# A finer-grained opening: 128-token pieces, half products ahead of the scores, and class-1 norms drained in three parts

## Chip, cores and metric

The kernel runs on 1 core of one Trainium2 chip. The metric is the device time of one execution in microseconds (us), lower is better, as the median of several executions. The kernel before takes 1280.66 us (three executions, 1279.89 to 1280.86).

## The reference

Two layers, each an attention block followed by a token-mixing MLP, with layer norms without weights, in bf16. Cut to what matters here:

```python
x = A_x                                  # 1 x 2048 tokens x 1024
for layer in range(2):
    h = layernorm(x)
    q, k, v = split(h @ wqkv)            # 32 heads of 32
    # 8 keys per query, 2 tokens apart: tokens t, t-2, ..., t-14 (masked below 0)
    logits = einsum("hsd,hswd->hsw", q, kg) * scale
    x = x + (softmax(logits) applied to vg) @ wo
    h = layernorm(x)
    x = x + MLP over the token axis(h)   # w1, gelu, w2, biases
```

The dilation of 2 splits the tokens into two classes that never meet in attention: even tokens (class 0) and odd ones (class 1), 1024 tokens or eight tiles of 128 each.

## The kernel before: the parts that matter

TensorE is the engine that is nearly always busy. The program fixes the order of each engine's instructions when it is built, and in the traces below an engine stands at an instruction whose operand isn't ready (1.24 us at 39.65 in the kernel before) rather than taking a later one. The schedule: two pieces of code make it.

The first is the opening: eight class-0 tiles are loaded, normed, transposed on TensorE ("turn"), copied from PSUM ("place"), and projected to q and k. Matmuls of the identity ("idle") fill TensorE meanwhile, for the sake of its clock: in the trace the first eight start about 0.43 us apart, the last eight about 0.21.

```python
        idle(16)
        moments(0)            # statistics on VectorE, 1/sqrt on ScalarE
        own_sum(0)
        moments(1)
        norm(0)
        turn(0)
        idle(3)
        # ... (cut: tiles 1 to 3, then the first projections, 256 tokens at a time)
        for u, i in (((1, 0), 2), ((1, 1), 3), ((0, 0), None)):
            banks[u] = bank()
            project(*u, 0, banks[u], 0, 2 * P)
```

Scores: for each feature tile, q times the shifted k on VectorE (the product T, 128x4096), which TensorE then sums over features with a selection matrix (the "sc" matmuls). In the first group of scores each T is followed by its own sum:

```python
            for par in range(2):
                ...
                T = self.t_buf(n, dq, par)
                mult = nc.vector.tensor_tensor(out=T, in0=q..., in1=window(k, ...), op=ALU.mult)
                ...
                if not joined:
                    self.qk_sum(dq, par, T)
```

The second piece weaves other work into this lead stream while the program is built. `second` is the class-1 norms (eight pieces), `v_ahead` the v projections of class 1 (sixteen pieces of 8 matmuls), `out0` the first output projection, and so on. The weave keeps its own count of TensorE and VectorE time, `pe` and `dve`, and pulls filling pieces in where that count says that TensorE would otherwise wait:

```python
    def weave(lead, fills, lags):
        ...
                u = next(fills[f], None)
                if u is not None:
                    pe = max(pe, opened[f]) + u[0]
                    dve += u[1]
                    return True
                del opened[f]
                when[f] = pe + lags.get(f, 6.0)        # the fill has ended: what follows it may open
                for x, y in (("out0", "partials"), ("out0", "late"), ("second", "v_ahead")):
                    if f == x and y in opened:
                        opened[y] = when[f]
        ...
            elif kind == "drain":
                while unit[0] in opened:               # all that is left of this fill, here and now
                    pull(True)
        ...
        weave(lead, {"second": second_class(), "v_ahead": v_ahead(), "out0": ..., ...},
              {"second": 25.0} if first else {})
```

In the stream of the attention:

```python
            yield from lead if lead is not None else qk_proj(0, 0)      # the opening
            yield "open", "second"
            if lead is not None:
                yield "drain", "second"                                 # all eight class-1 norms
            yield "open", "v_ahead"
            for n in range(last + 1):                                   # scores, softmax, p*v ...
```

Weights come through a pool of five buffers (`wbp`), which the v projections and the output projection share.

## Time and profile before

| | before |
|---|---|
| median | 1280.66 us (1279.89 to 1280.86) |
| profiled span | 1278.8 us, granted clock 1.0 |
| TensorE busy | 98% |
| TensorE idle in 0-12 / 12-34 / 34-60 / 60-180 / 180-242 us | 3.7 / 0.2 / 1.5 / 0.7 / 2.8 us |
| first projection / end of the first six | 11.98 / 25.61 us |
| first scores / second | 37.80 / 39.65 us (1.24 us of waiting before the second) |

The idle times are the length of a stretch less its "PE" column in the view by stage. The prediction shows that view, the waits and the order of work, so they aren't repeated here. One habit is needed for the rest: a row of the timeline reads "start, length, engine, line, operation, output<-inputs, shapes, count", and the bracket is the idle time of that engine just ahead of the row with what ended it.

### The profile page before, as it was taken

To read this page: it belongs to the slowest core of one execution; us is meant where nothing else is said; L and a number is where in the kernel's file an instruction comes from. 1 tells how busy PE (TensorE), PEld (TensorE's weight loads), DVE (VectorE), ACT (ScalarE), POOL (GpSimd) and SP (SyncE) were. 2 spreads that over 40 slices of the span, in tenths; PEclk is the share of its full clock that TensorE was granted. 3 is DMA by queue.
4 is the path that set the end of the run, shared out by engine and by line. 5 is a ranking of instruction groups with operands and counts; after the bars stand their busy time and mean duration, and the time that the engine had idled before them with its cause. 6 is when DMAs were issued, how large, how long until landed. Compare 5 with 4: busy or idle time off the path is not lost.

```text
span 1278.8 us, 15455 instructions
## 1 busy us (share of the span) xinstructions
PE 1258.0 (98%) x6163; PEld 577.4 (45%) x6284; DVE 689.9 (54%) x869; ACT 489.3 (38%) x812; POOL 61.3 (5%) x166
## 2 busy tenths in 40 slices
PE   8999999999999999999999999999999999999998
PEld 4344444444444444444444444444444444444444
DVE  6789999999114322334798834899930233111011
ACT  6845446634424533324533445453352343000000
POOL 3000000001000000000000000010010000000000
PEclk9999999999999999999999999999999999999999
DMA  9853454553422289952738542358262223344331
GB/s 256 190 124 106 99 139 142 171 143 115 132 83 83 64 220 305 291 161 87 187 103 201 152 124 80 83 159 207 66 181 83 82 67 89 107 128 135 99 115 52
DMA packets 217817, 173.00 MB, mean 135 GB/s; under 512 B 32081, under 2 KB 198353, under 8 KB 215697
## 3 DMA queue, kind: packets, MB, share of 16 engines
q1 hardware_dynamic: 206768, 126.11, 36.5%
q0 software_dynamic: 9248, 37.51, 10.5%
q10 hardware_dynamic: 1728, 8.39, 1.7%
q8 instruction: 49, 0.80, 0.3%
q14 instruction: 24, 0.19, 0.0%
HBM read 139.47 MB, written 26.21 MB: 130 GB/s over the span
## 4 chain that ended last, share of the span: by engine, by line
PE 76%; DVE 5%; issue 2%; ACT 1%; DMA 0%; DVEq 0%
PE ps L719 30%; PE ps L743 29%; PE ps L418 11%; PE ps L664 4%; DVE T L456 2%; PE sc L480 1%; DVE pr L538 1%; DVE pr L543 1%; DVE xr L689 0%; ACT h L227 0%; ACT h L238 0%; DMA wo<-in_A_wo_dram 0%; DVE v L545 0%; DVE xr L692 0%; ACT ln L200 0%
## 5 line engine op out<-in xcount | busy, mean ns | idle before, releaser
L719 PE MATMUL ps<-h,w 128*128 128x512 bf16 x1754 | 385.6, 379 | 4.0 <-ACT h L238 2.0
L743 PEld LDWEIGHTS <-w 128*128 128x128 bf16 x1820 | 177.6, 98 | 209.9 <-issue 2.1
L719 PEld LDWEIGHTS <-w 128*128 128x128 bf16 x1792 | 175.2, 98 | 214.1 <-issue 3.4
L418 PE MATMUL ps<-hT,wq 128*128 128x512 bf16 (+1 forms) x1087 | 240.2, 374 | 2.5 <-issue 0.6
L743 PE MATMUL ps<-g,w 128*128 128x512 bf16 (+1 forms) x1017 | 225.9, 376 | 1.2 <-issue 0.2
L743 PE MATMUL ps<-gg,w 128*128 128x512 bf16 (+1 forms) x766 | 170.9, 376 | 0.9 <-issue 0.2
L418 PEld LDWEIGHTS <-wq 128*128 128x128 bf16 x1112 | 109.1, 100 | 128.8 <-issue 9.1
L748 DVE SCALAR_TENSOR_TENSOR xr<-ps,b_sb,xr 128x512 bf16<-128x512 f32 (+1 forms) x65 | 45.5, 738 | 225.1 <-PE ps L743 182.6
L456 DVE TENSOR_TENSOR T<-q,k 128x4096 bf16<-128x4096 bf16 x44 | 99.0, 2284 | 70.5 <-ACT q L422 52.4
L543 DVE TENSOR_TENSOR pr<-pr 128x2048 bf16<-128x2048 bf16 (+1 forms) x128 | 119.4, 949 | 0.3
L730 DVE TENSOR_TENSOR tmp<-ps,gg 128x512 f32<-128x512 f32 x48 | 33.2, 692 | 150.2 <-PE ps L719 148.2
L418 PE MATMUL ps<-hT,wv 128*128 128x512 bf16 x436 | 99.5, 380 | 0.6
L664 PE MATMUL ps<-wo,oT 128*128 128x512 bf16 x377 | 88.6, 379 | 1.1 <-DVE oT L545 0.7
L425 ACT CAST k<-ps 128x1024 bf16<-128x1024 f32 x60 | 60.7, 1014 | 61.0 <-PE ps L418 59.0
L538 DVE TENSOR_TENSOR pr<-pb,v 128x2048 bf16<-128x2048 bf16 x64 | 75.9, 1218 | 10.8 <-ACT v L425 6.1
L538 DVE TENSOR_TENSOR pr<-pb,g 128x2048 bf16<-128x2048 bf16 x64 | 76.6, 1216 | 7.6 <-DMA pb<-pd 5.1
L418 PEld LDWEIGHTS <-wv 128*128 128x128 bf16 x448 | 48.9, 111 | 48.7 <-issue 4.2
L730 DVE TENSOR_TENSOR tmp<-ps,g 128x512 f32<-128x512 f32 x48 | 33.2, 692 | 49.7 <-PE ps L719 46.9
L664 PEld LDWEIGHTS <-oT 128*128 128x128 bf16 x384 | 37.3, 98 | 46.8 <-issue 1.2
L422 ACT CAST q<-ps 128x512 bf16<-128x512 f32 x60 | 34.9, 586 | 49.5 <-PE ps L418 49.5
L731 ACT ACTIVATE gg<-tmp,b_sb 128x512 bf16<-128x512 f32 x48 | 34.6, 721 | 49.9 <-DVE tmp L730 49.9
L731 ACT ACTIVATE g<-tmp,b_sb 128x512 bf16<-128x512 f32 x48 | 34.6, 721 | 43.5 <-DVE tmp L730 43.1
(97 smaller groups left out, 755.9 us busy)
## 6 DMA issues: line engine op xcount, KB each, us to landing
w<-in_B_w_dram SPq DMA_DIRECT2D x56, 512.0 KB, 4.8
w<-in_B_w_dram SPq DMA_DIRECT2D x64, 448.0 KB, 3.8
wq<-in_A_wqkv_dram SPq DMA_DIRECT2D x38, 512.0 KB, 4.3
pb<-pd POOLq DMA_DIRECT2D x16, 1024.0 KB, 8.7
wo<-in_A_wo_dram SPq DMA_DIRECT2D x16, 512.0 KB, 3.9
xa<-xr POOLq DMA_DIRECT2D x32, 256.0 KB, 3.4
xr<-xa SPq DMA_DIRECT2D x32, 256.0 KB, 4.0
wv<-in_A_wqkv_dram SPq DMA_DIRECT2D x14, 512.0 KB, 5.4
```

The costliest lines, as they stand in the source:

```text
L418: nc.tensor.matmul(ps[:, lo:hi], lhsT=cols, rhs=self.hT[c][hf][:, kt, lo:hi], start=(kt == 0), stop=(kt == KD - 1))
L422: nc.scalar.copy(out=self.q_of(c, dt)[:, hf * HT:(hf + 1) * HT], in_=ps[:])
L425: nc.scalar.copy(out=window(buf, 0, PADK + hf * HT, [(KW + 1, 2), (1, HT)]), in_=ps[:].unsqueeze(1).to_broadcast([P, 2, HT]))
L456: mult = nc.vector.tensor_tensor(out=T, in0=q.unsqueeze(1).to_broadcast([P, 4, SC]), in1=window(k, par, 2, [(2, 4), (1, SC)]), op=ALU.mult)
L538: mult = nc.vector.tensor_tensor(out=pr[:, :, u, :], in0=pb[:, :, u, :], in1=window(self.v_of(c, dt), par, 2 + hf * HT, [(TB, 4), (2, 4), ...
L543: nc.vector.tensor_tensor(out=pr[:, :, 0:wd, :], in0=pr[:, :, 0:wd, :], in1=pr[:, :, wd:2 * wd, :], op=ALU.add)
L664: nc.tensor.matmul(banks[(i, n)][:], lhsT=at_.oT[c][kt][:, i * P:(i + 1) * P], rhs=wo_t[n][kt // 4][:, kt % 4, :], start=(kt == 0), stop=( ...
L719: nc.tensor.matmul(ps[:], lhsT=wt[c][:, i, fl * P:(fl + 1) * P], rhs=h2[c][i // 4][:, i % 4, dc * 512:(dc + 1) * 512], start=(k == 0), sto ...
L730: nc.vector.tensor_tensor(out=tmp[:], in0=ps[:], in1=gs, op=ALU.add)
L731: nc.scalar.activation(out=gs, in_=tmp[:], func=ACT.Gelu_apprx_tanh, bias=b1_sb[:, ft:ft + 1])
L743: nc.tensor.matmul(ps[:, 0:xc.stop - xc.start], lhsT=w2t(ft, c), rhs=g[ft // GF][:, ft % GF, xc], start=(ft == 0), stop=(ft == FT - 1))
L748: nc.vector.scalar_tensor_tensor(out=xo[:, xc], in0=ps[:, 0:xc.stop - xc.start], scalar=b2_sb[:, i, c:c + 1], in1=xo[:, xc], op0=ALU.add, ...
```

## The change

The intent: start TensorE's useful work earlier by handing it smaller pieces, make the first q*k products in halves before the class-1 norms occupy VectorE, and place the class-1 norms in three parts between the first scores, so that the scores don't stand behind all of them. The core of the diff, with cuts:

```diff
-        idle(16)
-        moments(0)
-        own_sum(0)
-        moments(1)
+        idle(14)
+        stats(0, 0)
+        stats(0, 1)
+        root(0)
+        stats(1, 0)
         norm(0)
         turn(0)
 ...
+        for u in ((1, 0), (1, 1)):
+            project(*u, 0, banks[u], 0, P)          # 128 tokens as soon as tile 0 is there
 ...
+        for dq, par in AHEAD_T:                     # three half products
+            ahead(0, dq, par, HT)
```
```diff
             yield "open", "second"
             if lead is not None:
-                yield "drain", "second"
+                for dq, par in AHEAD_T:
+                    self.multiply_ahead(0, dq, par, SC)
+                yield from self.qk(0, 0)
+                for u in ((1, 3, 1), (0, 2, 0)):
+                    yield from self.proj(0, *u)
+                self.multiply_ahead(0, 1, 1, SC)
+                for u in ((0, 2, 1), (0, 3, 0), (0, 3, 1)):
+                    yield from self.proj(0, *u)
+                yield "drain", "second", NT // 2    # four of the eight norms
             yield "open", "v_ahead"
 ...
                     yield from self.qk(n, 2 * half + 1)
+                    if lead is not None and n == 0:
+                        yield "drain", "second", NT // 4   # two more, twice
 ...
             elif kind == "drain":                          # in the weave: a drain can have a number
-                while unit[0] in opened:
+                for _ in range(unit[1]) if unit[1:] else iter(int, 1):
+                    if unit[0] not in opened:
+                        break
                     pull(True)
```
```diff
         def opening():
-            for i in range(NT):
-                x_stage(0, i)
-            load_biases()
+            x_stage(nc.sync, 0, 0, slice(0, P // 2))       # tile 0 in halves, two queues
+            x_stage(nc.scalar, 0, 0, slice(P // 2, P))
+            x_stage(nc.scalar, 0, 1)
+            x_stage(nc.sync, 0, 2)
+            at_.weights(0, 1, 0)                           # first weights ahead of later tiles
 ...
                 for i in range(NT):
-                    x_stage(1, i)
+                    x_stage(nc.gpsimd, 1, i)
+                load_biases()
```

In the weave itself only the drain changes: it now takes a number of pieces, and 4 + 2 + 2 are all eight.

## The prediction

> **What bounds the kernel now.** I read the page first, then the busy time of the engines by stage, then the waits of TensorE over the whole span, then the order of work on TensorE and VectorE in the first 60 us. The page says that one engine holds the span:
>
> ```profile
> PE 1258.0 (98%) x6163; PEld 577.4 (45%) x6284; DVE 689.9 (54%) x869; ACT 489.3 (38%) x812; POOL 61.3 (5%) x166
> ```
>
> TensorE is busy for 1258.0 of 1278.8 us. A change that removes no real matmul can win only what TensorE spends idle or on filling, so I looked for both by stage (columns: stretch, its length, then PE, PEld, DVE, ACT, POOL busy, clock, DMA share, GB/s):
>
> ```profile
> 0.00:12.00 12.00, 8.28 (x41) 3.46 (x42) 7.32 (x18) 5.52 (x16) 7.57 (x61) 1.00 0.92 265
> 12.00:34.00 22.00, 21.80 (x157) 13.20 (x160) 14.32 (x30) 16.18 (x36) 4.69 (x10) 1.00 1.05 258
> 34.00:60.00 26.00, 24.46 (x151) 9.51 (x153) 20.36 (x14) 24.21 (x57) 0.00 (x0) 1.00 0.93 206
> 60.00:180.00 120.00, 119.26 (x633) 56.34 (x643) 110.59 (x111) 63.37 (x71) 3.36 (x6) 1.00 0.41 110
> 180.00:242.00 62.00, 59.21 (x313) 25.79 (x319) 60.23 (x78) 38.66 (x81) 6.05 (x11) 1.00 0.58 166
> 242.00:540.00 298.00, 296.52 (x1354) 135.01 (x1380) 130.88 (x198) 116.45 (x186) 9.87 (x18) 1.00 0.57 156
> ```
>
> The undisturbed stretch (242 to 540) loses 1.5 us in 298, 0.5%. Above that rate the idle time is 3.7 us in the first 12, 1.4 in 34 to 60, next to nothing in 60 to 180 although VectorE is 92% busy there, and 2.5 in 180 to 242. The rest lies in the second layer and at the tail, behind 300 us of unbroken matmuls, where this change cannot reach. The waits name what ends the idle time (us in total, times, longest):
>
> ```profile
> PE sc L480 <- DVE T L456: 3.4, 9, 1.2
> PE ps L719 <- ACT h L238: 2.0, 2, 1.2
> PE tp L290 <- DVE gg L233: 1.8, 2, 1.2
> PE ps L261 <- POOL ident masks.py:199: 1.6, 1, 1.6
> ```
>
> The TensorE rows of the opening show that even its busy time is largely filling (start, length, what, idle before it):
>
> ```profile
> 1.57 5.30 PE L261 MATMUL ps<-ident 128*128 128x512 bf16 x16 [1.57 <-POOL ident masks.py:199]
> 8.06 0.62 PE L290 MATMUL tp<-ident,gg 128*128 128x128 bf16 x8 [1.19 <-DVE gg L233]
> ...
> 10.36 1.24 PE L261 MATMUL ps<-ident 128*128 128x512 bf16 x5
> 11.98 1.03 PE L418 MATMUL ps<-hT,wq 128*128 128x256 bf16 x8 [0.38 <-ACT t L281]
> ...
> 25.61 7.07 PE L418 MATMUL ps<-hT,wq 128*128 128x512 bf16 x31
> ...
> 39.65 0.61 PE L480 MATMUL sc<-T,sel 128*32 128x512 bf16 x8 [1.24 <-DVE T L456]
> ```
>
> The L261 rows multiply the identity and throw the result away. The first projection starts at 11.98 us; before it only two tiles' transposes (about 0.45 us each) are useful, so some 11 us of this case are dead time at the start. From 11.98 to 25.61 us TensorE has no gap: all of tiles 0 to 7 turned, and the first-half projections of six feature tiles, take 13.6 us. The 1.24 us at 39.65 is the one real hole before 60. VectorE in the same time:
>
> ```profile
> 4.63 1.29 DVE L267 BATCH_NORM_STATS2 bn<-gg 128x6 f32<-128x512 bf16 x2 [3.73 <-DMA gg<-in_A_x_dram]
> ...
> 27.47 1.29 DVE L207 BATCH_NORM_STATS2 bn<-gg 128x6 f32<-128x512 bf16 x2 [2.69 <-DMA gg<-in_A_x_dram]
> ...
> 35.05 2.27 DVE L456 TENSOR_TENSOR T<-q,k 128x4096 bf16<-128x4096 bf16 x1
> ...
> 49.51 8.89 DVE L456 TENSOR_TENSOR T<-g,g 128x4096 bf16<-128x4096 bf16 x4 [1.39 <-ACT g L422]
> ```
>
> It waits for the first token tile until 4.63, idles at 24.8 to 27.5, and does its first q*k product only at 35.05, after all the class-1 statistics. So the product is late, not slow.
>
> **What the Trainium skill says.** "TensorE: Matmul & The Clock Gate", section "What's actually happening": the array starts at half clock and gets the full one after some 3.4 us of activity. The trace agrees: the first eight fillers take from 1.57 to about 5.0 us, 0.43 us each, and the remaining eight about 0.21. Fourteen instead of sixteen therefore still end warm, near 6.4 us (6.87 less 0.43), and the holes that I expect afterwards are far below 3.4 us. "DMA: Bandwidth & Descriptors", section "Rules for kernel authors", says of two transfers to disjoint partition halves "Don't bother — they serialize", since both use the same 16 engines. I agree for bandwidth; here the split is about order: tiles 0 and 1 now travel side by side on two queues and land together, and two halves of tile 0 travel ahead of tile 1. No run shows it yet. The same section says that a strided last dimension lowers to one descriptor per element. The bias loads are such: 11 KB that took 10.5 and 9.6 us to land, and between 11 and 16 us the DMA engines are full (1.26) but move only 104 GB/s, against 366 from 4 to 8 us. "VectorE: DVE Perf Modes", section "Side-by-side: where the cycles go for N=2048 bf16", gives a fixed part of about 0.15 us for an instruction; the trace agrees, 1.216 us for a bf16 product of 2048 a partition and 2.284 for 4096, so a split costs 2 x 1.216 - 2.284 = 0.15 us of VectorE.
>
> **The change part by part.**
>
> *First tile and weights.* The tile's halves go first on both queues, and the first weights third on their queue rather than fifth. By the bytes moved in each us of before (0.04 MB by 2 us, 0.23 by 3, 0.53 by 4, 0.90 by 5, 1.29 by 6, 1.66 by 7), 0.25 MB has passed at 3.1 us, against tile 0 and tile 1 together (0.5 MB) at 3.9. Before, the landing was seen at 4.63, about 0.7 later than the bytes; I take 0.4 of the 0.8 us, because the second queue started late (nothing before 2.0 us): tile 0 at 4.2. The first weights were issued at 2.61 and landed about 8.3 us later, at 10.9; after, behind 1.0 MB plus their own 0.5, at about 7.5. Weights are then no bound.
>
> *Chain to the first projection, after (estimate from the durations of before).* Statistics 4.2 to 5.5, aggregate to 5.7, Ln and Exp to 6.3, one half of the next tile's statistics beside them, norm 6.35 to 6.9 (before, a whole second tile's 1.4 us stood ahead of it), transposes to 7.5, the next tile's root on ScalarE, copy 8.15 to 9.15. Projection of 128 tokens at 9.25 instead of 256 at 11.98: 2.7 us earlier, of which the halving gives about half, as it no longer waits for tile 1's copy.
>
> *What is given back.* The early projections outrun the tiles: the second piece needs tile 1 copied by ScalarE, at about 11.4 by the same counting, and TensorE has 10.15 to 11.45 to fill with 0.45 us of tile 2's transposes. Hole: 0.85. Then it is fed: two 128-token pieces, two 256-token pieces, transposes, four second halves, tiles 4 to 7, two more projections, which end at about 23.4 by summing 0.055 us for each 128 columns. A 128-token matmul costs half of a 256-token one (transposes of 128 show eight in 0.44 us, the 256-token group eight in 0.88), so the pieces add no streaming time. Against 25.61 this is 2.2 us; for a wait on ScalarE's order (root, copies, own sum, square and norm of tile 4 in one queue) I take off 0.3: **1.9 us**.
>
> *Products ahead.* Three half products of 1.22 us come before the class-1 tiles land, in the 2.7 us that VectorE idled; the other halves follow as q and k arrive. Four splits cost at most 0.6 us of VectorE, none of TensorE. At the first score TensorE finds its T finished: the 1.24 us hole goes, **1.2 us**.
>
> *Norms in three parts.* The same instructions, in between products. VectorE's work from 24 to the end of the first eight products is about 8 us of norms and 18 of products, so they can end near 50 us instead of 58.4: up to 8 us of lead for VectorE, TensorE's own gain being about 3. This lead serves only where TensorE runs out of filling, that is in 180 to 242, where it waited for a VectorE oT (0.7), a T (0.3) and a ScalarE h that hangs on VectorE sums (1.2). I count a quarter of the 2.2: **0.5 us**.
>
> *Biases later.* Their DMA jam moves from 11-16 us to about 28-33, after the class-1 tiles. It meets transposes and weights with over 10 us in hand: 0.
>
> Sum: 1.9 + 1.2 + 0.5 = 3.6 us, 1280.66 - 3.6 = 1277.1.
>
> **The rivals.**
> *The opening is given back.* ScalarE's queue becomes the bound of the opening: copies of tiles 0 and 1 (1.0 each), and tile 4's path (about 5 us) before the evacuations. With six PSUM banks, four held by open projections, a transpose could wait for an evacuation behind it. For it: ScalarE had only 0.6 us of slack at several places up to 20 us. Against: the transposes of before never waited for an evacuation. Then gain 0.5 from the start, 1.2 from the hole: about 1279.
> *Filling runs short.* Class 1 is finished later, and with it the v projections that fill TensorE at 63 to 130 us. If VectorE's lead and this delay leave a hole of 1 to 3 us, the time is 1279 to 1281. Against: the q/k and v projections ready by then are 21 us of work, and 60 to 180 has no hole today.
> *More than I count.* If the lead removes all of the 2.2 us after 180, and tile 0 lands at 3.9: 1274.8.
> *A slower clock.* If the shorter filling let the clock fall, each 3.4 us at half clock would cost 1.7; the holes are too short.
>
> **Range and chances.** The sum has 1.5 us of uncertainty from the opening and 2 from the stretch after 180, since every later order shifts. 8 times in 10 between 1274.4 and 1280.2. A 2% change would be 25.6 us, over twice all the dead time at the start; a loss of that size would need a new stall that nothing here suggests: faster 0.005, same 0.99, slower 0.005.
>
> **What would show it.** The first projection near 9.3 us and the end of the sixth near 23.4; the first statistics near 4.2; no wait of a score matmul for T near 40 us; first product before 27.5; VectorE's eighth product ending near 50; the 180-242 idle time at 2.3 us or less; 60-180 still full. I am wrong if the start gains under 1 us, if a hole opens between 60 and 130, or if the idle time after 180 grows.

## The result, and the profile after

| | before | after |
|---|---|---|
| median | 1280.74 us (6 runs, 1279.89 to 1281.09) | 1287.87 us (6 runs, 1283.58 to 1291.76) |
| granted clock of the runs | 1.0 in all | 0.995 to 1.0 |
| profiled span | 1278.8 us | 1287.6 us |

The ratio is 1.0056, 95% interval 1.0036 to 1.0077. A ratio is the mean time of one kernel's fast runs over that of the other's fast runs of the same rounds, so it isn't quite the ratio of the two medians. The change costs some 7 us where the prediction said that it gains 3.6. The scatter grew too: two of the six runs had the full clock throughout and took 1283.58 and 1286.70, so the clock alone doesn't explain the loss.

The page's first line looks like the one of before, although the span is 8.8 us longer (1287.6 against 1278.8). A share of the whole span hides what happened:

```profile
PE 1258.1 (98%) x6188; PEld 579.3 (45%) x6309; DVE 690.3 (54%) x872; ACT 490.2 (38%) x812; POOL 61.2 (5%) x166
```

The view by stage of the kernel after, to be held against the same stretches in the prediction (stretch, length, then PE, PEld, DVE, ACT, POOL busy with their counts, granted clock, DMA share, GB/s):

```profile
0.00:12.00 12.00, 7.76 (x53) 3.92 (x54) 6.84 (x16) 5.10 (x11) 4.87 (x59) 1.00 0.86 258
...
34.00:60.00 26.00, 24.24 (x142) 10.01 (x146) 19.64 (x22) 25.20 (x60) 0.41 (x2) 1.00 1.14 214
60.00:180.00 120.00, 114.65 (x610) 53.60 (x621) 111.67 (x110) 59.69 (x68) 3.97 (x7) 1.00 0.40 105
180.00:242.00 62.00, 56.87 (x292) 24.72 (x297) 56.66 (x75) 36.90 (x72) 5.42 (x10) 0.94 0.58 151
```

60 to 180 us, which was full before (119.26 of 120), now has 5.35 us of idle TensorE; 180 to 242 us has 5.13 instead of 2.79, and a clock of 0.94. 34 to 60 us, where a hole was to close, is no fuller (24.24 against 24.46). Narrower stretches say where: first the kernel before,

```profile
60.00:105.00 45.00, 44.68 (x239) 21.32 (x241) 39.65 (x38) 23.32 (x27) 1.71 (x3) 1.00 0.37 91
180.00:200.00 20.00, 19.18 (x87) 8.36 (x87) 20.00 (x26) 7.50 (x18) 2.80 (x5) 1.00 0.67 170
```

and then the kernel after:

```profile
60.00:105.00 45.00, 40.65 (x230) 18.86 (x234) 41.48 (x36) 20.45 (x25) 1.69 (x3) 1.00 0.44 115
180.00:200.00 20.00, 15.91 (x61) 7.02 (x62) 16.10 (x21) 6.90 (x12) 1.61 (x3) 0.83 0.88 198
```

TensorE loses 4.0 us in the first and 3.3 us in the second, and in the second the clock is 0.83. TensorE's waits over the whole span of the kernel after name the releasers (us in total, times, longest):

```profile
PE sc L527 <- DVE T L505: 4.0, 9, 1.6
PE ps L719 <- DMA wo<-in_A_wo_dram: 4.0, 1, 4.0
PE sc L527 <- DVE gg L505: 4.0, 3, 1.6
```

Before, the first of these was 3.4 and the other two weren't on the list: a wait for the weights of the output projection (wo), and three waits of the second and third score groups for their products (gg is a buffer that such a product lies in). In order of time, first TensorE of the kernel before at the second score group and ahead of the first output projection,

```profile
72.46 1.05 PE L480 MATMUL sc<-gg,sel 128*32 128x512 bf16 x16
...
77.01 1.05 PE L480 MATMUL sc<-gg,sel 128*32 128x512 bf16 x16
...
169.36 13.77 PE L418 MATMUL ps<-hT,wq 128*128 128x512 bf16 x61
182.97 4.48 PE L664 MATMUL ps<-wo,oT 128*128 128x512 bf16 x20
188.12 9.67 PE L664 MATMUL ps<-wo,oT 128*128 128x512 bf16 x43 [0.67 <-DVE oT L545]
```

and then TensorE of the kernel after:

```profile
10.24 1.06 PE L447 MATMUL ps<-hT,wq 128*128 128x128 bf16 x16
...
24.21 7.08 PE L447 MATMUL ps<-hT,wq 128*128 128x512 bf16 x31
...
45.31 0.61 PE L527 MATMUL sc<-T,sel 128*32 128x512 bf16 x8 [1.60 <-DVE T L505]
...
72.82 1.05 PE L527 MATMUL sc<-gg,sel 128*32 128x512 bf16 x16 [1.09 <-DVE gg L505]
...
97.81 1.05 PE L527 MATMUL sc<-gg,sel 128*32 128x512 bf16 x16 [1.60 <-DVE gg L505]
...
178.97 7.07 PE L447 MATMUL ps<-hT,wv 128*128 128x512 bf16 x31
185.87 4.48 PE L719 MATMUL ps<-wo,oT 128*128 128x512 bf16 x20
194.34 6.70 PE L719 MATMUL ps<-wo,oT 128*128 128x512 bf16 x18 [3.99 <-DMA wo<-in_A_wo_dram]
```

The first row is the first projection; the second starts where the first six end. They are 1.74 and 1.40 us earlier than before. The hole among the first scores is still there, at 45.31 instead of 39.65, and longer. And at 178.97 stand 32 matmuls of class-1 v projections (7 us of work), where the kernel before has none: it was through with them at 168.2. VectorE of the kernel after, for the three things that the prediction said of it:

```profile
4.12 1.29 DVE L268 BATCH_NORM_STATS2 bn<-gg 128x6 f32<-128x512 bf16 x2 [3.23 <-DMA gg<-in_A_x_dram]
...
24.07 1.22 DVE L505 TENSOR_TENSOR T<-q,k 128x2048 bf16<-128x2048 bf16 x1
...
27.70 1.21 DVE L505 TENSOR_TENSOR T<-q,k 128x2048 bf16<-128x2048 bf16 x1
...
42.97 8.90 DVE L505 TENSOR_TENSOR T<-g,g 128x4096 bf16<-128x4096 bf16 x4 [0.33 <-ACT g L451]
```

The first statistics are 0.51 us earlier, the first product (a half one, at 24.07; the second is at 27.70) 10.98 us earlier, and the last of the first eight products ends at 51.87 instead of 58.40. VectorE did get its lead. It didn't help. Last, the stretch around the wo wait:

```profile
190.00:192.50 2.50, 0.35 (x2) 0.07 (x1) 2.50 (x7) 0.00 (x0) 0.00 (x0) 1.00 1.26 277
192.50:199.40 6.90, 5.06 (x13) 1.75 (x13) 3.17 (x4) 2.27 (x7) 0.59 (x1) 0.51 0.71 162
```

TensorE stops at 190.35 for want of wo. From 192.5, some 2.1 us into the wait, the granted clock is 0.51, and it stays there until 199.4: 5.06 us of busy time at half speed, so about 2.5 us lost on top of the 3.99.

The account between the two traces: 4.0 us in 60-105, 0.6 in 105-140, 3.3 + 2.5 in 180-200, -0.9 in 200-242 (idle 1.04 instead of 1.96) and 1.4 in 242-600, in all 10.9. Against it stands the lead that TensorE has at the v projections after the first q/k block, which begin at 61.64 instead of 63.55: 1.9. That makes 9.0; the spans differ by 8.8.

### The profile page after: what moved, and what is told of

It is laid out like the page before. It is cut to its first block, busy times and chain, and to the rows that moved or that the text cites. A ratio compares the mean times of both kernels' runs of the same rounds, so it can differ in the third digit from the quotient of the medians.

```text
span 1287.6 us, 15511 instructions
## 1 busy us (share of the span) xinstructions
PE 1258.1 (98%) x6188; PEld 579.3 (45%) x6309; DVE 690.3 (54%) x872; ACT 490.2 (38%) x812; POOL 61.2 (5%) x166
## 4 chain that ended last, share of the span: by engine, by line
PE 82%; DVE 7%; issue 4%; DMA 4%; ACT 3%; POOL 0%; DVEq 0%; POOLq 0%
PE ps L774 29%; PE ps L798 29%; PE ps L447 17%; PE ps L719 5%; DVE pr L585 2%; DVE T L505 2%; DVE pr L590 2%; PE sc L527 1%; DMA b_bf<-in_B_b_dram 1%; DMA wo<-in_A_wo_dram 1%; DVE gg L505 1%; DMA wv<-in_A_wqkv_dram 1%; ACT h L229 1%; ACT h L240 1%; DMA pb<-pd 1%
## 5 line engine op out<-in xcount | busy, mean ns | idle before, releaser
L447 PE MATMUL ps<-hT,wq 128*128 128x512 bf16 (+2 forms) x1112 | 239.4, 370 | 2.8 <-DMA hT<-hb 1.0
L505 DVE TENSOR_TENSOR T<-q,k 128x4096 bf16<-128x4096 bf16 (+1 forms) x45 | 97.3, 2191 | 72.7 <-ACT q L451 53.1
L447 PE MATMUL ps<-hT,wv 128*128 128x512 bf16 (+1 forms) x443 | 99.5, 376 | 1.3 <-DMA wv<-in_A_wqkv_dram 0.6
L719 PE MATMUL ps<-wo,oT 128*128 128x512 bf16 x379 | 91.6, 387 | 4.4 <-DMA wo<-in_A_wo_dram 4.0
```

The costliest lines, as they stand in the source:

```text
L447: self.last_mm = nc.tensor.matmul(ps[:, lo:hi], lhsT=cols, rhs=self.hT[c][hf][:, kt, lo:hi], start=(kt == 0), stop=(kt == KD - 1))
L505: return nc.vector.tensor_tensor(out=T[:, :, lo:hi], in0=q[:, lo:hi].unsqueeze(1).to_broadcast([P, 4, hi - lo]), in1=window(k, par, 2 + lo ...
L719: nc.tensor.matmul(banks[(i, n)][:], lhsT=at_.oT[c][kt][:, i * P:(i + 1) * P], rhs=wo_t[n][kt // 4][:, kt % 4, :], start=(kt == 0), stop=( ...
```

## The experiments

**Theory A.** The three-part drain changes the weave's own count (the program's bookkeeping, not a time on the chip). Printing it while the two programs are built shows two steps. The last class-1 norm is placed at 42.3 instead of 32.25. And since the three drains take just the eight pieces, the end of the norms is noticed only when the weave next looks for filling, at 63.3. So `when["second"]` is later, and `v_ahead` opens at 88.3 instead of 57.25, 31 us later. (The expectations speak of 10 us; that is the first step alone.) TensorE's instruction order, which can be read from the built program without running it, shows the consequence. Around the second score group (number of matmuls : output<-inputs, sc for the score sums; hT class 1 are the class-1 activations):

```
before  16:ps<-hT class 0,wv  8:ps<-hT class 1,wv  16:sc  16:ps<-hT class 1,wv  16:sc  64:ps<-hT class 0,wq ...
after   16:ps<-hT class 0,wv                       16:sc   9:ps<-hT class 0,wq  16:sc  55:ps<-hT class 0,wq ...

before  64:ps<-hT class 1,wq                                     64:ps<-wo,oT
after   64:ps<-hT class 1,wq  32:ps<-hT class 1,wv               39:ps<-wo,oT  16:sc  25:ps<-wo,oT ...
```

(The buffer names are replaced by the classes, and the second pair of lines is the stretch ahead of the first output projection.) Filling is missing where the scores wait for VectorE, and stands where nothing needs it; there it keeps weight buffers, so the last wo load comes late, TensorE waits, and its clock drops.

**Rival B.** The new opening itself costs: VectorE and ScalarE are disturbed by the split products and the moved loads, and the loss follows from that.
**Rival C.** The late loads collide on the DMA, and the order plays no part.

The first four kernels separate A from B. All experiments ran with five timed rounds; the kernel before took 1280.42, 1280.61, 1280.56 and 1280.41 us (medians).

### The three-part drain alone, in the kernel before

```diff
             yield "open", "second"
-            if lead is not None:
-                yield "drain", "second"
             yield "open", "v_ahead"
 ...
                     yield from self.qk(n, 2 * half)
+                    if lead is not None and n == 0 and half == 0:
+                        yield "drain", "second", NT // 2
                     yield from self.qk(n, 2 * half + 1)
+                    if lead is not None and n == 0:
+                        yield "drain", "second", NT // 4
```

> The kernel before with one part of the change alone: the class-1 norms drained in three parts between the first scores (4, 2 and 2 of 8). Theory A (the later end of that drain opens the class-1 v projections 10 us later in the program's own ordering, so four of them are missing as filling between 70 and 105 us and stand at 180 us instead, where they also hold the weight buffer that the last output-projection tile wo needs): 1285 to 1291 us, TensorE idle 60 to 180 above 4 us, and a wait of about 4 us on the wo load near 190. Rival B (the products ahead and their buffers make the holes) and rival C (the new opening with its later bias loads makes them): 1280 to 1281, as before.

Measured: 1287.03 us (six runs, 1284.14 to 1291.31), ratio 1.0053 (1.0039 to 1.0066). None of the new opening is in this kernel, and it has the whole loss, with the scatter. Its `v_ahead` opens at 88.3 in the weave's count too. Two of its stretches:

```profile
60.00:105.00 45.00, 41.64 (x237) 19.18 (x236) 40.70 (x36) 20.49 (x24) 1.70 (x3) 1.00 0.48 125
180.00:200.00 20.00, 17.14 (x82) 7.76 (x84) 16.92 (x23) 7.78 (x13) 2.03 (x4) 0.91 0.90 203
```

and TensorE's row after its wo wait:

```profile
193.86 5.62 PE L666 MATMUL ps<-wo,oT 128*128 128x512 bf16 x19 [2.85 <-DMA wo<-in_A_wo_dram]
```

The same two places are short of work, by 3.4 and 2.9 us, and the clock falls after the same wait. Rival B isn't needed for the loss.

### The change with one drain

```diff
             if lead is not None:
+                yield "drain", "second"
                 for dq, par in AHEAD_T:
 ...
-                yield "drain", "second", NT // 2
 ...
-                    if lead is not None and n == 0:
-                        yield "drain", "second", NT // 4
```

> The changed kernel with the norms drained in one go before the first scores, as before; the opening by pieces and the products ahead stay. Theory A: the order of TensorE from 63 us on is that of before again, the wo wait is gone and the idle time from 60 to 180 under 1.5 us, and what the opening wins shows: 1277 to 1280. Rivals B and C: 1285 to 1291, as the changed kernel.

Measured: 1282.41 us (1281.40 to 1283.67), ratio 1.0016 (1.0004 to 1.0028). 5.5 of the 7.4 us between this run's before-time and the changed kernel's median come back, but the new opening's gain doesn't show. The trace says why: 60-105 is nearly full again (44.24 of 45), but the score hole is now 2.42 us, ahead of 37.63, and the clock is half from 38.5 to 41.9. So there is a second loss, in 34-60, which theory A doesn't cover.

### The new opening alone, without products ahead, one drain

```diff
-    AHEAD_T = ((0, 0), (0, 1), (1, 0))
+    AHEAD_T = ()
 ...
+                yield "drain", "second"          # and the stream as in the kernel before
```

> The new opening alone (pieces, DMA order, later biases), without products ahead and with one drain. Theory A: the opening's 1.4 us shows nearly whole, 1278.5 to 1280. Rival C (opening and its DMA order are the cause of the loss): 1285 or more. If the opening's gain is lost later for lack of anything to do: 1280.5.

Measured: 1282.09 us (1280.41 to 1283.09), ratio 1.0007 (0.9994 to 1.0020): nothing gained. TensorE begins its first scores at 36.56 instead of 37.80, and the second ones stand where they stood before (TensorE's row):

```profile
39.59 0.70 PE L525 MATMUL sc<-T,sel 128*32 128x512 bf16 x8 [2.42 <-DVE T L503]
```

Its stretches before and after that row:

```profile
36.00:40.00 4.00, 1.58 (x19) 0.43 (x17) 4.00 (x7) 4.00 (x10) 0.70 (x1) 1.00 1.27 200
40.00:43.40 3.40, 3.40 (x12) 1.18 (x9) 3.40 (x3) 3.40 (x14) 2.20 (x1) 0.50 1.09 241
```

39.59 against 39.65: an earlier TensorE only waits longer, and 2.42 us of waiting was enough for 3.4 us at half clock, which gives back about 1.7 us more. The runs at full clock took 1280.41, 1280.88 and 1282.29, so the clock isn't all of it.

### The change with the lag at zero

Theory A says that one constant undoes the loss with all of the change in place.

```diff
-              {"second": 25.0} if first else {})
+              {"second": 0.0} if first else {})
```

> The changed kernel whole, drain in three parts kept, but the class-1 v projections allowed as soon as the norms are done in the program's ordering (delay 0 instead of 25 us). Theory A: four of them fill TensorE before 80 us, none is left at 180, wo loads early: 1276 to 1280. Rival B or C: 1285 to 1291.

Measured: 1280.50 us (1278.23 to 1282.45), ratio 0.9997 (0.9985 to 1.0009): 7.4 us below the changed kernel, by one number that moves v projections forward in TensorE's order (`v_ahead` opens at 63.3 in the count). 60 to 180 us is full, and no wo wait is left:

```profile
60.00:180.00 120.00, 120.00 (x646) 56.37 (x644) 105.72 (x103) 63.45 (x70) 3.33 (x6) 1.00 0.41 112
180.00:200.00 20.00, 19.33 (x91) 8.55 (x90) 19.86 (x29) 4.97 (x13) 2.79 (x5) 1.00 0.65 157
```

What seems to keep it from gaining is a score hole of 2.96 us ahead of 47.06, after which the clock is 0.50 from 48.0 to 51.4 in the profiled run.

### The change with the last wo weights in a buffer of their own

This splits the loss: it leaves the order as the change has it, and takes only the shortage of weight buffers away.

```diff
-                wt = wb("wo", [P, KD // 2, 512])
+                if (at_.li, c, n, hf) == (0, 0, 1, 1):
+                    wt = g_two[-1][:, 0:KD // 2 * 512]...      # a buffer idle at this time
```

> The changed kernel with the fourth wo tile of the first output projection put in a buffer that is idle then, so that its load no longer waits for a late class-1 v projection to free a weight buffer; TensorE's order of work is unchanged but for the buffer's name. Theory A in two parts (holes from 60 to 105 us cost 4 to 5 us; the late wo, 4 us of wait and up to 2.6 us of half clock behind it, is a second cost): 1281 to 1285, no wo wait, holes before 105 us as in the changed kernel. If the wo wait only takes the place of a wait that would come anyway: 1286 to 1289.

Measured: 1284.35 us (1284.06 to 1289.13; four of five runs within 0.4 us, all four at full clock), ratio 1.0036 (1.0022 to 1.0049).

```profile
60.00:105.00 45.00, 40.63 (x231) 18.87 (x233) 40.62 (x35) 20.94 (x24) 1.69 (x3) 1.00 0.45 117
180.00:200.00 20.00, 18.72 (x98) 8.74 (x99) 19.81 (x25) 9.80 (x16) 2.16 (x4) 1.00 0.96 217
```

The wo wait and the clock drop behind it are gone, and 3.5 us with them (1287.87 - 1284.35), and most of the scatter. The missing filling in 60-105 is as it was (40.63 against 40.65), and the 3.7 us left over the kernel before are put down to it. The split is rough: the two ratios' intervals overlap, and one of the changed kernel's own six runs, at full clock, took 1283.58, no more than this version does. So the price of the wo wait differs from run to run. This also answers rival C: the DMA share in 180-200 is higher here (0.96) than in the changed kernel (0.88), without a wait. What delayed wo was when its load could be issued. The last wo load was issued at 185.20 in the changed kernel, once the late v projections released their buffer, and took 9.1 us beside two 1 MB loads; before, the last of the three in this stretch was issued at 167.4 and none took more than 5.1.

### The lag at 35 in the kernel before

The reverse of the lag of zero: delay `v_ahead` in a kernel that has none of the change, by 10 us (to 67.25 in the weave's count), a third of what the change does.

```diff
-              {"second": 25.0} if first else {})
+              {"second": 35.0} if first else {})
```

> The kernel before with one number changed: the delay after the norms at which class-1 v projections are allowed in the program's ordering, 35 in place of 25 us. Norms, products and opening stay as before. Theory A (the order of the v projections is the cause, not where the norms stand on VectorE and ScalarE): 1282 to 1286; a part of the loss only, as the order keeps two units of eight early. If the place of the norms itself is the cause: 1280 to 1281.

Measured: 1295.12 us (four runs, 1292.42 to 1295.75), ratio 1.0106 (1.0091 to 1.0122). The direction is A's, the size isn't: more than twice the expected loss, and more than the change's own, from a smaller delay. Here a second weight load comes late as well:

```profile
133.50 11.37 PE L418 MATMUL ps<-hT,wv 128*128 128x512 bf16 x43 [4.22 <-DMA wv<-in_A_wqkv_dram]
...
201.09 4.00 PE L664 MATMUL ps<-wo,oT 128*128 128x512 bf16 x9 [3.98 <-DMA wo<-in_A_wo_dram]
```

So the loss doesn't grow with the delay: the order is found anew each time, and what the late pieces then hold up differs. But late v projections alone, without any change of norms or products, make the same wo wait.

### Two k projections among the first scores

If idle TensorE among the first scores can be filled, ready work must stand there. Two projections of a later feature pair are put ahead of the third feature tile's scores, on top of the lag of zero.

```diff
+    EARLY = ((1, 4, 0), (1, 5, 0))
 ...
+                    if lead is not None and nx == (0, 1):
+                        for u in EARLY:
+                            yield from self.proj(0, *u)
```

(The same units are left out where they stood. They are the k projections of feature tiles 4 and 5, first token half, and they read class-0 activations; where an expectation calls them class-1, that is a slip.)

> The changed kernel with delay 0 and with the next two k projections placed before the third feature tile's scores, so that TensorE has work in the hole at 44 to 47 us. If that hole (3.0 us in the delay-0 profile, with 3.4 us of half clock behind it) is what eats the opening's gain: 1276 to 1278.5 and less scatter, faster than before; if the opening's gain is lost elsewhere: 1280 to 1282.

Measured: 1278.29 us (1277.57 to 1279.23, all at full clock), ratio 0.9983 (0.9970 to 0.9995). This is the first version below the kernel before, by 2.3 us. The 2.96 us hole became one of 0.31 and one of 1.52 us (ahead of 48.01 and 52.20), short enough to keep the clock.

### The new opening with three q projections ahead of the first scores

```diff
+                yield "drain", "second"
                 for u in ((0, 2, 1), (0, 3, 0), (0, 3, 1)):
                     yield from self.proj(0, *u)
```

(On the new opening without products ahead.)

> The new opening alone, one drain, no products ahead, with the three class-0 q projections moved ahead of the first scores, so that TensorE does not stand at the second score waiting for VectorE (2.4 us at 37 in the opening-alone profile, then 3.4 us of half clock). If that hole is where the opening's 1.4 us went: 1278 to 1279.5 and no low clock; if not: 1280.5 to 1282.

Measured: 1281.03 us (1280.56 to 1282.03), ratio 1.0004 (0.9992 to 1.0017): a miss. The clock stayed up, but the hole only moved: 0.56 us ahead of 46.07 and 1.58 ahead of 53.15, and VectorE waited 4.17 us at 43.23 for a 1/sqrt of ScalarE. In the profiled run the sixth projection ended at 25.05, hardly earlier than before.

### The first tile whole, on one queue

```diff
-            x_stage(nc.sync, 0, 0, slice(0, P // 2))
-            x_stage(nc.scalar, 0, 0, slice(P // 2, P))
+            x_stage(nc.sync, 0, 0)
```

(On the version with two early k projections.)

> The best version so far (new opening, lag of 0 for the second group, two class-1 k projections ahead of the third feature tile's scores: 1278.29 us) with the first token tile loaded whole on one queue instead of in halves on two. If the halves bring the first data earlier and the chain at the start carries it, the first statistics come 0.3 to 0.5 us later than with halves and the time is 1278.4 to 1278.9. If the later score stage absorbs the start (VectorE bound there), 1278.3 all the same, with a shorter hole before the second score group.

Measured: 1277.66 us (1277.55 to 1278.00), ratio 0.9977 (0.9964 to 0.9989). The halves aren't needed. The first statistics come at 4.61 us, 0.5 later than with halves, but tile 1's follow without a wait (6.06, against 6.29 after 0.66 of waiting), and the first projection is at 9.78 against 9.93. Over all traces of kernels with the new opening, the first projection lies between 9.87 and 11.07 with halves (ten traces) and between 9.70 and 9.89 with the whole tile (four). In the same traces the first statistics start between 4.08 and 4.98 with halves and between 4.52 and 4.71 with the whole tile, tile 1's between 6.14 and 7.42 and between 5.97 and 6.16. This is the fastest and steadiest version, 2.9 us below the kernel before (1280.56). That it beats the version with halves isn't proven: their intervals overlap.

### Four early k projections instead of two

```diff
-    EARLY = ((1, 4, 0), (1, 5, 0))
+    EARLY = ((1, 4, 0), (1, 5, 0), (1, 4, 1), (1, 5, 1))
```

> The best version so far with four early class-1 k projections instead of two. If the holes of 1.52 and 0.31 us that are left among the first scores are idle TensorE time that any ready work fills, 1276.6 to 1277.6. If VectorE and ScalarE are the bound of this stretch, the hole only moves later and the time stays at 1278.0 to 1278.6.

Measured: 1279.61 us (1277.41 to 1280.83), ratio 0.9986 (0.9972 to 0.9999). In the profiled run 34 to 60 is full (26.00 of 26), and a hole of 1.03 us stands ahead of the second score group at 72.97 instead. That run also started late (tile 1's statistics at 7.40, first projection at 11.04). The five runs lie in two groups, 1277.4 to 1277.6 and 1279.6 to 1280.8; whether the start explains the upper group isn't shown.

### The reorderings without the change

```diff
                     if lead is not None and nx == (0, 1):
-                        for u in ((0, 2, 1), (0, 3, 0), (0, 3, 1),):
+                        for u in ((0, 2, 1), (0, 3, 0), (0, 3, 1)) + EARLY:
 ...
-              {"second": 25.0} if first else {})
+              {"second": 0.0} if first else {})
```

(On the kernel before.)

> Control: the kernel before, whose opening stays, with the lag of 0 and the two early k projections alone. If the gain of the best version is due to the reordering, 1278.0 to 1279.0. If it is due to the new opening, which needs the reordering only so as not to lose what it gained, 1280.0 to 1281.0.

Measured: 1280.94 us (1280.46 to 1281.19), ratio 1.0001 (0.9989 to 1.0014). So the four corners are: neither 1280.6, the change alone 1287.9, the reordering alone 1280.9, both 1278.3. The gain of the last is the change's own; the reordering only keeps it from being thrown away.

### The bias rows loaded early again

```diff
             for i in range(5, NT):
                 x_stage(nc.sync, 0, i)
+            load_biases()
             clear_pads()
 ...
-                load_biases()
```

(On the version with two early k projections.)

> The best version so far with the bias rows loaded and cast early, as the kernel before has them. If moving them was neutral, 1278.3 within 0.4. If the GpSimd cast beside the VectorE products (up to 4.41 us long in one run) slows the score stretch, 1277.3 to 1277.9. If the early transfer delays the first tiles, 1278.7 to 1279.3.

Measured: 1279.02 us (1277.92 to 1279.35), ratio 0.9985 (0.9973 to 0.9998). The median lies in the third range, that of an early transfer that delays the first tiles, and in the trace the first projection is at 10.47 instead of 9.93. But the runs overlap with those of 1278.29, so a cost isn't shown. What the pair does show is what the bias rows do to the DMA: from 11 to 16 us it moved 127 GB/s with them and 318 GB/s without, at a busy share of 1.32 and 1.16. Moved late, they show the same at 33 to 38 us (136 GB/s at a busy share of 1.23, against 166 at 0.64). One descriptor per element, the prediction's reason for it, can't be seen there: in the kernel before, the trace counts 112 packets on their queue for the 11 KB. The trace shows one more side effect: moved late, the small bias conversion on GpSimd took 0.21 us in the changed kernel but 4.41 us in the version with one drain, where it fell beside VectorE products; loaded early it took 0.21. It's off the path, and no run shows that it cost anything.

### Class-1 norms moved between ScalarE and VectorE

By then it was shown why the change loses, but not why the 1.24 us hole never closes. In 34-60 us both VectorE (about 20 of 26 us) and ScalarE (24 to 26) are heavily used, and VectorE's waits point at ScalarE. ScalarE norms tiles 1, 3, 5 and 7 of class 1. Three kernels on the version with the whole first tile shift that balance. They aren't clean tests: each edit also changes what the norm pieces tell the weave (2 us of VectorE for a tile that VectorE norms, 0 for the others; that line is cut here), so the order of the v projections moves too. In TensorE's row just ahead of the second score group stand 48 v matmuls with four tiles on ScalarE, and 64, 56 and 40 with two, three and five.

```diff
     def prologue_tile(c, i, hT):
         t = staged(c, i)
-        if i % 2:                 # four of the eight on ScalarE
+        if i in (1, 5):           # two
```

> The version with the whole first tile (1277.66 us), with ScalarE norming two of the eight class-1 token tiles instead of four (tiles 3 and 7 go to VectorE, about 2.0 us of VectorE work each, and take some 4.9 us each off ScalarE). If ScalarE is the bound from 34 to 60 us, the 1.16 us hole at 51 shrinks or goes and the time is 1276.3 to 1277.3. If VectorE is the bound, it gets 4 us more, the hole grows by 1 to 3 us and the time is 1278.5 to 1280.5.

Measured: 1283.12 us (1282.40 to 1287.80), ratio 1.0030 (1.0018 to 1.0042).

```diff
+        if i in (1, 3, 5):        # three
```

> The same with three of the eight on ScalarE (only tile 7 moved). ScalarE bound: 1276.7 to 1277.5. VectorE bound: 1278.0 to 1279.0.

Measured: 1279.38 us (1279.28 to 1280.27), ratio 0.9994 (0.9982 to 1.0006).

```diff
+        if i % 2 or i == 6:       # five
```

> The other way: tile 6 moved from VectorE to ScalarE, so five of the eight on ScalarE. ScalarE bound: holes grow by 2 to 5 us in sum, perhaps with a low clock after them: 1279.0 to 1283.0. VectorE bound: 1276.5 to 1277.5.

Measured: 1282.61 us (six runs, 1279.97 to 1289.73), ratio 1.0028 (1.0006 to 1.0050). The stretch from 34 to 60 with two tiles on ScalarE,

```profile
34.00:60.00 26.00, 21.72 (x121) 8.15 (x120) 20.17 (x25) 16.19 (x39) 0.45 (x2) 0.87 1.08 200
```

and with five,

```profile
34.00:60.00 26.00, 26.00 (x153) 10.80 (x152) 16.28 (x15) 26.00 (x67) 0.41 (x2) 1.00 0.97 204
```

whose next hole on TensorE is this:

```profile
71.55 1.90 PE L528 MATMUL sc<-gg,sel 128*32 128x512 bf16 x16 [3.14 <-DVE gg L506]
```

My leading guess, ScalarE as the bound of the first scores, isn't confirmed, and VectorE isn't shown to be the bound either. For VectorE: with two tiles on ScalarE (16.19 us busy) the holes grow, to 2.17 and 2.12 us, and the clock falls; with five, VectorE is relieved (16.28 us busy) and the hole among the first scores is gone altogether, 26.00 of 26. Against it: with three tiles VectorE norms one tile more than with four, and yet the early holes shrink, from 1.16 us to 0.67 in sum (1.09 us opens ahead of 168.18 instead). And with four, VectorE itself waited 1.44 us for a 1/sqrt of ScalarE at 48.20, ahead of the product that the 1.16 us hole (ahead of 51.00) waits for.

With five tiles ScalarE has no gap left, VectorE waits 7.03 us for its copy of the scores, and 3.14 us of hole open at the second score group, with half clock after it. Eight v matmuls fewer stand ahead of that group than with four tiles, some 1.75 us of work, so a part of this hole is the order's. Of the expectations, five tiles came out in the range for ScalarE as the bound, two and three tiles in neither range. The two engines share this stage, and each split that was tried moved the hole; which of them bounds it stays open.

### Halves again, on the version with two tiles on ScalarE

The edit is the reverse of that of the whole first tile.

> The run with two tiles on ScalarE, with the first token tile again in halves on two queues, the one difference. If the halves gain the 0.4 us of the prediction, 0.3 to 0.5 us below that run. If what tile 0 gains is lost at tile 1, the median is the same or up to 1 us higher and the runs scatter over more than 1 us, against under 0.5 with the whole tile.

Measured: 1284.66 us (1283.61 to 1286.60), ratio 1.0034 (1.0021 to 1.0047), against 1283.12 with the whole tile on the same chip. No gain of 0.4 shows in either pair. The scatter expected of the halves doesn't show against this base, which scatters itself through the clock.

## Why the prediction was wrong, point by point

*Norms in three parts.* This is the step that failed. It said "The same instructions, in between products", counted VectorE's lead and gave +0.5 us. VectorE's lead came (6.5 us), and where the prediction hoped for its use, in 200-242, TensorE's idle time did fall by 0.9 us. But the step followed only what the diff moves, not what the moved `drain` sets: the counter from which the weave opens the class-1 v projections, 88.3 instead of 57.25. With it TensorE's order changed from 60 to 186 us, and that cost about 7 us: about 3.5 for the wo wait and its clock drop (the kernel with wo's own buffer), some 3.7 for the filling missing at the second and third score groups. Shown by the drain alone (1287.03) and by the lag of zero (1280.50).

*The rival "Filling runs short".* It named the right mechanism, the delayed v projections, and was put aside with "the q/k and v projections ready by then are 21 us of work". Work that is ready doesn't help an engine that runs in a fixed order; it has to stand at that place in the queue. The size was also too small: 1 to 3 us of hole were foreseen, 4.6 came in 60-140. The load that comes late because late pieces hold its buffer wasn't foreseen at all.

*The rival "The opening is given back".* It put the loss on ScalarE's queue. In the opening-alone kernel the lead did reach the end of the sixth projection (24.37 us); it was lost at the second score, in a hole of 2.42 us and the half clock after it. The sum of *More than I count* is off: its own terms (1.7 us more after 180, 0.3 at the start) give 1275.1, not 1274.8.

*Products ahead.* "At the first score TensorE finds its T finished: the 1.24 us hole goes". True of the first scores, which don't wait (32.94 us), though only one of the three half products came before the first class-1 statistics (24.07; the others at 27.70 and 28.83). The hole moved to the fifth product and is 1.60 us long in the changed kernel, up to 2.96 in others. The step looked at one product and not at the queue behind it, in which the norms now stand: from 38.55 to 42.64 us VectorE worked on norms, and the fifth product starts at 42.97.

*Opening.* 1.9 us were predicted and 1.4 measured at the end of the sixth projection (24.21; with the whole tile 23.75). The mechanism held: smaller pieces, first projection 1.74 us earlier against a predicted 2.7. The first statistics at 4.12 were as predicted (4.2), but half of the next tile's statistics then waited 0.94 us for their data, which wasn't in the count, and no run shows a gain from the halves.

*A slower clock.* "the holes are too short" is refuted. In the changed kernel the drop came 2.1 us into the wo wait, and four of its six runs were touched. The length of a hole alone doesn't decide: one of 2.12 us was followed by half clock, one of 2.17 us wasn't. In the 16 traces that have clock records, the granted clock changes only at steps of 3.41 us. Cut into such windows, the traces give a plain picture (the idle time of a window is 3.41 less its "PE" column). The lag at 35, whose 4.22 us hole ends at 133.50:

```profile
127.80:131.21 3.41, 1.47 (x7) 0.57 (x5) 3.41 (x4) 1.02 (x1) 0.51 (x1) 1.00 1.01 211
131.21:134.63 3.42, 1.13 (x6) 0.62 (x7) 3.42 (x3) 0.04 (x1) 0.00 (x0) 1.00 1.16 321
134.63:138.04 3.41, 3.41 (x10) 1.21 (x9) 3.41 (x4) 1.22 (x2) 0.00 (x0) 0.50 0.94 205
```

The hole lies across two windows. After 1.94 us of idle time in the first the clock stays; after 2.28 in the second it falls, when the hole is already over. The two nearest to the border are one of two tiles on ScalarE with halves,

```profile
46.16:49.57 3.41, 1.35 (x12) 0.43 (x11) 3.41 (x4) 1.44 (x4) 0.00 (x0) 1.00 1.10 315
49.57:52.99 3.42, 2.46 (x12) 0.72 (x12) 3.42 (x3) 1.14 (x2) 0.00 (x0) 0.50 1.08 207
```

and one of the opening with three q projections:

```profile
5.01:8.42 3.41, 1.44 (x7) 0.47 (x5) 2.12 (x5) 0.50 (x2) 1.43 (x26) 1.00 1.05 327
8.42:11.84 3.42, 2.50 (x33) 1.89 (x34) 3.31 (x8) 2.33 (x7) 0.00 (x0) 1.00 1.13 338
```

Over these traces, all ten windows at full clock with 2.06 to 2.80 us of idle time were followed by half clock, and none with 1.98 us or less was. So in this case a hole can cost clock from about 2.1 us on, and how it falls across the windows decides. The prediction's 1.24 us hole was safe; the waits that the change made weren't.

*Biases later: 0.* Held within what these runs can tell.

*Range.* 1274.4 to 1280.2 left out a loss, although the prediction listed "if a hole opens between 60 and 130" as what would make it wrong. That is what happened, and the idle time after 180 grew as well (2.79 to 5.13 us in 180-242), another of its signs. The class "same" was right.

Open: why the lag at 35 costs more than the change; which engine bounds the first scores; why the early four k projections give two groups of runs; and whether a finer split of single norms could close the hole in 34-60 without opening one behind it.

## What to carry to other kernels

When a change moves a marker in a program that builds its own order (a drain, a priority, a lag), compare the order of the bound engine's whole queue before and after, not only the moved instructions: here one unmoved constant of 25 decided over 7 us, and two thirds of the shift came from a drain that took all the pieces without noticing the end. Early work gains only as far as the next bound that it meets; take the gain at the first point where another engine paces this one, and check that a longer wait there doesn't cost the clock. Filling that is placed late can be worse than absent filling, since it holds buffers that the next weights need.

## What the Trainium skill lacked or had wrong

- "TensorE: Matmul & The Clock Gate", section "What's actually happening", gives the slow clock as following at least one idle window of about 3.4 us. The lows here do last 3.41 us or twice that, but the window ahead of them wasn't idle throughout: 2.06 to 2.80 us of idle time in it were followed by half clock in all ten cases, 1.98 us or less in none. To take a hole as safe because it is well below 3.4 us, as the prediction did, was wrong from about 2.1 us on.
- "DMA: Bandwidth & Descriptors", section "Rules for kernel authors", was right against the prediction: "Don't bother" about two partition halves. What it lacks is the effect on order: in one pair the halves brought the first tile 0.5 us earlier (4.10 against 4.61; in the other 4.69 against 4.71) and the second one later (6.29 against 6.06), with no gain in time (1278.29 against 1277.66, and 1284.66 against 1283.12).
